# Attention in phases of 12 and 14 scores, with copies of scores and one arena of slots

## The chip, the cores and the metric

The kernel runs on one core of a Trainium2 chip. The metric is the device time of one execution in microseconds (us); smaller is better. Five engines work side by side, each with its own queue of instructions in order: TensorE (PE, the matmuls; PEld is its load of weights), ScalarE (ACT), VectorE (DVE), GpSimd (POOL) and SyncE (SP, which here starts the DMAs). They wait for one another through semaphores, and the queue of an engine never overtakes: what stands behind a waiting instruction waits too. TensorE writes to PSUM, a memory of eight banks of 128 x 512 floats; here seven of them hold scores and sums and one the second layer.

## The reference

Attention with 32 heads of 16 dimensions over 2048 tokens, and a token-mixing MLP, mixed by a gate:

```python
x = A_x                                                  # (1, 2048, 512)
g = sigmoid((x * gate_w).sum(-1, keepdims=True))
qkv = (x @ wqkv).reshape(B, S, 3, 32, 16).transpose(2, 0, 3, 1, 4)
p = softmax(einsum("bhqd,bhkd->bhqk", q, k) * 16 ** -0.5)
a = einsum("bhqk,bhkd->bhqd", p, v).transpose(0, 2, 1, 3).reshape(B, S, 512) @ wo
u = gelu(einsum("bsd,sf->bdf", layernorm(x), w1) + b1)   # F = 1792
b = (einsum("bdf,fs->bds", u, w2) + b2).transpose(0, 2, 1)
return g * a + (1 - g) * b
```

## The kernel before, in words

In front of the attention stand the layer norm, the projections to q, k and v and the MLP's first layer. They run at full array rows. Then comes the attention, three quarters of the time, and the MLP's second layer runs inside it. At the end stands a short stage of last outputs. All float32 products but the scores and AV are split in a high and a low part, three matmuls each.

The attention's work is counted in *units*. A unit is one score matmul (L868) of 128 keys by 512 queries of one head: it uses only 64 of the array's rows. On the other 64 rows a half of a second-layer or output matmul runs at the same time (L989, the list `beside`; its result is the bank `dn`). The scores land in one bank of PSUM, ACT takes their exponential and writes it to SBUF (`exponential`, L891), and `apply_v` (L826, here called AV) multiplies by V: two matmuls a unit, recorded as four instructions, all of a phase into one bank, which DVE then adds to the sums of the group in SBUF (L846, `ot`). The softmax's denominator comes out of AV as one more column, and the sums are divided at the end.

There are 32 groups of 64 units. The loop (L941 to L1017) goes through them in 8 phases of 8 units each, 256 phases in all. In a phase PE issues eight scores, six or eight of them with a partner, then AV of the *previous* phase's units; ACT takes two single exponentials and three of two banks each. `TURN` says for each of three kinds of phase which score goes to which of the seven banks, which exponentials are taken together, and which bank AV uses. In 21 groups one pair of scores is not given to ACT: DVE copies and scales it (L931) and computes the exponential in a polynomial, a few steps a phase (L907 to L920). DVE also carries out steps from the list `slow` (splits, divisions) where a phase has room. A memset on POOL (`token`, L993) in each phase keeps the order of the partners.

Nothing is left to a scheduler: the order on each queue is the order of the program. Waits come from what the framework tracks of the tiles; all seven banks are one tile, `banks`. Two functions add to that and take from it: `reads` and `writes` order an instruction behind those that last wrote or read its bank, and declare that there is no dependence on recent instructions that read another bank.

The output projection of the first half of the tokens is done in two passes of six matmuls: the first goes to DRAM (`part_d`) and is read again for the second.

Of the kernel before, what the change touches and what calls it, by code (L numbers as in the profile page):

```python
# [22 lines left out]
P = 128  # L23
# [52 lines left out]
def gated_mix(ctx: ExitStack, tc: tile.TileContext, a_x, a_wqkv, a_wo, b_w1, b_b1, b_w2, b_b2, gate_w, out):  # L76
# [415 lines left out]
    o_pool = ctx.enter_context(tc.tile_pool(name="o", bufs=1, reuse_waits="tile"))  # L492
    att_ctx = ExitStack()
    stk = att_ctx.enter_context(tc.tile_pool(name="stk", bufs=2, reuse_waits="tile"))
# [33 lines left out]
    def second_out(t, ps):  # L528
# [8 lines left out]
    QC = NB // 2  # L537

# [5 lines left out]
    TURN = [  # L544
# [3 lines left out]
    ]  # L548
# [4 lines left out]
    ptp_ctx = ExitStack()  # L553
    ptp = ptp_ctx.enter_context(tc.tile_pool(name="pt", bufs=7, reuse_waits="tile"))
# [3 lines left out]
    o_parts = {}  # L558
    wo_hi = o_pool.tile([P, ND, D], F32R, name="wo_hi")
    wo_lo = o_pool.tile([P, ND, D], F32R, name="wo_lo")  # L560
# [29 lines left out]
    def load_wo(k):  # L590
        raw = o_pool.tile([P, D], F32, name="o_sum")
        nc.sync.dma_start(raw, a_wo[k * P : (k + 1) * P, :])
        parts = wo_hi[:, k, :], wo_lo[:, k, :]
        slow.append((two + 1, lambda: split(*parts, raw, nc.vector.tensor_copy, nc.vector.tensor_tensor)))
# [6 lines left out]
    def open_end():  # L601

        nonlocal end
        u_ctx.close()
        wk_ctx.close()
        end = end_ctx.enter_context(tc.tile_pool(name="end", bufs=1, side="right", reuse_waits="tile"))

        least.append(end.tile([P, 1], F32, name="least"))
        nc.vector.tensor_reduce(least[0], ident.rearrange("p (j r) -> p j r", r=32)[:, :, DH], axis=AX.X, op=ALU.add)
        nc.vector.tensor_scalar(least[0], least[0], -1.0, 3e38, ALU.add, ALU.mult)  # L610
        nc.vector.tensor_scalar_add(least[0], least[0], LEAST_SUM)

    def load_wq():
        wq.extend(end.tile([P, 2, D], F32R, name=f"wq{n}") for n in range(2))
        raw = end.tile([P, 2, D], F32, name="wq_raw")
# [5 lines left out]
        slow.append((two + 2, lambda: split(wq[0], wq[1], raw, nc.vector.tensor_copy, nc.vector.tensor_tensor)))  # L621

    def fetch_o(half, k, pairs=4):
# [3 lines left out]
        pool, name, bufs = (end, str(k), 1) if half else (o_pool, "", 2)  # L627
        hi = pool.tile([P, QW], F32R, name=f"o_hi{name}", bufs=bufs)[: n * DH]
        lo = pool.tile([P, QW], F32R, name=f"o_lo{name}", bufs=bufs)[: n * DH]
        raw, rb = lo.bitcast(F32), hi.bitcast(F32)  # L630
        nc.sync.dma_start(raw, o_d[half][k][: n * DH])
        nc.sync.dma_start(rb, r_d[half][k][:n, None, :].broadcast_to([n, DH, QW]))

        at = two + (1 if two + 2 == NG * TWOS else 2)

        def divide(i):
            cols = slice(i * NB, (i + 1) * NB)
            o = o_pool.tile([P, NB], F32, name="o_sum")[: n * DH]
            nc.vector.tensor_mul(o, raw[:, cols], rb[:, cols])
            split(hi[:, cols], lo[:, cols], o, nc.vector.tensor_copy, nc.vector.tensor_tensor)  # L640

        slow.extend((at, lambda i=i: divide(i)) for i in range(2))
        o_parts[half, k] = hi, lo

    def o_matmuls(half, t, n, m):

        cols = slice(t % 8 * P, (t % 8 + 1) * P)
        for i in range(n, m):
            k, j = divmod(i, 3)
            hi, lo = (x[:, cols] for x in o_parts[half, k])  # L650
# [10 lines left out]
    def project(t, n, m):  # L661
# [3 lines left out]
        def load():  # L665
            if m == EARLY:
                row = end.tile([P, D], F32, name=f"base{t}")
            elif end and t % 2:
                row = end.tile([P, D], F32, name="row", bufs=3)
            else:  # L670
                row = out_pool.tile([P, D], F32, name="row", bufs=3)
            rows[t] = load_row(row, part_d[t] if n else bp_d[t])

        def step(i):
            if i == 0:
                box.extend((ps_dn.tile([P, D], F32, name="dn"), list(o_matmuls(t // NH, t, n, m))))

            def done():
# [3 lines left out]
                elif m != EARLY:  # L682
                    nc.sync.dma_start(part_d[t], rows[t])

            return box[0], *box[1][i], i == 0, i == m - n - 1, done if i == m - n - 1 else None

        return [(step, i) for i in range(m - n)], load
# [4 lines left out]
    TWOS = 4  # L692
    N_S = 8
    dense, calls = {}, {}

    def put(steps, at, sizes):
        for n in sizes:
            dense[at] = [steps.pop(0) for _ in range(n)]
            at += 1
# [6 lines left out]
    def put_outputs(tiles, n, m, at):  # L706
        for t in tiles:
            steps, load = project(t, n, m)
            call(at - (2 if m > 6 else 1), load)
            at = put(steps, at, [m - n])  # L710
        return at

    EARLY = 8
    part_d = [dram.tile([P, D], F32, name=f"part{t}") for t in range(NS)]
    for k in range(ND):
        call(3 * k + 2, load_wo, k)
    steps = second_layer(0)
    first, at = steps[:28], put(steps[28:], 0, [8, 6])
    for t in range(1, NS):
        at = put(second_layer(t), at, [8, 6] * 3 if t in (7, 14, 15) else [6] * 7)  # L720
        if t == 7:
            call(at - 7, fetch_o, 0, 0)
            call(at - 3, fetch_o, 0, 1)
            at = put_outputs(range(NH), 0, 6, at)
    call(at - 11, fetch_o, 0, 2)
    call(at - 7, fetch_o, 0, 3)
    call(at, open_end)
    done, at = at, put_outputs(range(NH), 6, 12, at)
    at = put_outputs(range(NH, NS), 0, EARLY, at)

    for k, n in enumerate((1, 3, 4)):
        call(done + n, fetch_o, 1, k)
    call(done + 9, load_wq)
    assert at == NG * TWOS
    call((NG - 1) * TWOS + 2, fetch_o, 1, 3, 3)

# [8 lines left out]
    recent = deque(maxlen=10)  # L745
# [11 lines left out]
    def writes(mm, bank, block=0, source=None):  # L757
# [3 lines left out]
        for ins in recent:  # L761
            if ins not in readers[bank] and ins is not source:
# [6 lines left out]


    EXTRA = *range(0, 11), *range(15, 25)
    EXTRA_PH = 2

    DVE_ROOM = 2.45

    two = 0
# [15 lines left out]
    def invert_sums(half, k, pairs):  # L792
# [14 lines left out]
        wait = 1 if (half, k) == (1, ND - 1) else 3  # L807
        later(wait, invert)
        later(wait + 1, store)

    def apply_v(late, bank):

        if not late:
            return
        g, units = late
        pairs = list(zip(*([u for u in units if u[2] == qb] for qb in range(2))))
        assert 2 * len(pairs) == len(units)
        av = banks[:, bank, :]
        taken = [0, 0]

        for pair in pairs:
            for i, c, qb, pt, act in pair:
                taken[qb] += 1
                for h in range(2):
                    j = 2 * qb + h
                    mm = nc.tensor.matmul(  # L826
                        av[32 * j : 32 * j + VC, i * QC : (i + 1) * QC],
                        v[:, c, g % NP * 2 + i, :],
                        pt[:, h * QC : (h + 1) * QC],
                        start=taken[qb] == 1,  # L830
                        stop=taken[qb] == len(pairs),
                    )
                    writes(mm, bank, j, act)

        there = {(i, qb) for i, _, qb, *_ in units}
# [13 lines left out]
    with tc.manual_schedule(engines=engines):  # L849
        kt, qt = {0: load_k(0)}, {0: load_q(0)}  # L850
        late, fence = None, None
# [9 lines left out]
        pt = None  # L861

        def score(grp, i, n, turn, exps, units, apart):

            c, qb = n // 2, (n + i) % 2
            bank = turn[len(units)]
# [9 lines left out]
            units.append([i, c, qb, None, None])  # L876
            for which in exps:
                if which[-1] == len(units) - 1:
                    if which == apart:
                        steps_of_exp(turn, units, which)  # L880
                    else:
                        exponential(turn, units, which)

        def exponential(turn, units, which):
            nonlocal pt
            if which[0] != 1:
                pt = ptp.tile([P, 2, NB], F32, name="pt")
            which = sorted(which, key=lambda m: turn[m])
            first, at = which == [1], [turn[m] for m in which]
            dst = pt[:, first : first + len(at), :]  # L890
            act = nc.scalar.activation(dst, banks[:, at[0] : at[-1] + 1, :], AF.Exp, scale=SCALE)  # L891
            reads(act, *at)
            for n, m in enumerate(which):
                units[m][3:] = dst[:, n, :], act

        def steps_of_exp(turn, units, which):

            z = o_pool.tile([P, QW], F32R, name="o_hi", bufs=2).bitcast(F32).rearrange("p (n c) -> p n c", n=2)
            box = []
# [281 lines left out]
```

## Time and profile before

| | us |
|---|---|
| median of the 3 runs | 1278.32 |
| lowest and highest | 1278.27 to 1279.09 |
| span of the profiled execution | 1276.0 |
| PE busy in it | 1266.6 (99%) |
| ACT busy in it | 1071.9 (84%) |
| DVE busy in it | 719.3 (56%) |
| first score of the first phase at | 303.45 |
| first score of the last phase at | 1253.09 |

For the profiled execution the page gives the span alone, from the first to the last instruction; it has no time of its own beside that. A row of a timeline gives the start, the length, the engine, the line, the operation with its output and inputs, and in brackets how long the engine had been idle and what released it. Ends of matmuls are modelled: in a row of them each is shown longer than the distance to the next. A group's row gives its count, its busy time, the mean of one in ns, and the idle time before it with what ended it.

### The profile page before, as it was taken

How to read it: one execution, taken by the hardware profiler on the slowest of the kernel's cores; microseconds unless marked ns; L12 is line 12 of the kernel's file. 1: busy time of each engine (PE TensorE's matmuls, PEld its weight loads, DVE VectorE, ACT ScalarE, POOL GpSimd, SP SyncE). 2: the span in 40 equal slices, each digit the busy share in tenths (PEclk: the TensorE clock that was granted, in tenths of full speed). 3: DMA queues.
4: the chain of work that ended last, by engine and by line, in shares of the span. 5: the costliest groups of instructions: out<-in, count | busy, mean ns of one | idle time of the engine just before them, and what ended most of it. 6: DMA issues, size and time to landing. Idle time of an engine off the chain costs nothing.

```text
span 1276.0 us, 33051 instructions
## 1 busy us (share of the span) xinstructions
PE 1266.6 (99%) x13278; PEld 801.2 (63%) x13278; DVE 719.3 (56%) x1329; ACT 1071.9 (84%) x1484; POOL 210.8 (17%) x435
## 2 busy tenths in 40 slices
PE   9999999999999999999999999999999999999998
PEld 7888888886555555555555555555555555555555
DVE  5675363528776766666634346676666662325425
ACT  3444343437999999999999999999999999999994
POOL 0210144454111111111110011111111111100000
PEclk9999999999999999999999999999999999999999
DMA  4497743328443333433555533333343345446721
GB/s 133 141 304 274 241 122 99 99 71 166 84 93 59 74 76 70 79 70 76 116 107 115 129 77 69 69 72 76 68 78 72 74 82 109 98 88 198 149 62 70
DMA packets 94641, 137.37 MB, mean 108 GB/s; under 512 B 16313, under 2 KB 55375, under 8 KB 91408
## 3 DMA queue, kind: packets, MB, share of 16 engines
q1 hardware_dynamic: 93904, 134.14, 44.8%
q8 instruction: 106, 1.74, 0.6%
q10 hardware_dynamic: 576, 1.05, 0.2%
q14 instruction: 55, 0.45, 0.1%
HBM read 99.10 MB, written 36.03 MB: 106 GB/s over the span
## 4 chain that ended last, share of the span: by engine, by line
PE 99%; DMA 0%; ACT 0%; SPq 0%; DVE 0%; issue 0%
PE s L826 37%; PE s L868 34%; PE acc L429 12%; PE acc L90 10%; PE dn L989 4%; PE pa L1060 1%; PE acc L201 1%; PE dn L857 0%; PE acc L268 0%; DMA x<-in_A_x_dram 0%; ACT pt L891 0%; PE pa L1069 0%; SPq L193 0%; DVE base L1082 0%; SPq L186 0%
## 5 line engine op out<-in xcount | busy, mean ns | idle before, releaser
L891 ACT ACTIVATE pt<-s 128x512 f32<-128x512 f32 (+1 forms) x1259 | 943.5, 962 | 10.0 <-PE s L868 4.3
L868 PE MATMUL s<-qs,ks 64*128 64x512 f32 x2048 | 493.9, 404 | 0.8 <-POOL token L993 0.5
L826 PE MATMUL s<-pt,v 128*17 128x256 f32 x8024 | 482.6, 381 | 0.0
L868 PEld LDWEIGHTS s<-qs,ks 64*128 64x128 f32 x2048 | 325.4, 184 | 168.7 <-ACT pt L891 91.0
L846 DVE TENSOR_TENSOR ot<-s,ot 128x256 f32<-128x256 f32 (+2 forms) x427 | 190.4, 447 | 348.9 <-PE s L826 271.6
L826 PEld LDWEIGHTS s<-pt,v 128*17 128x17 f32 x8024 | 210.4, 97 | 232.2 <-ACT pt L891 84.2
L989 PE MATMUL dn<-u_hi,w_hi 64*128 64x512 f32 x428 | 186.4, 436 | 0.0
L83 POOL TENSOR_TENSOR w_lo<-w_raw,w_hi 128x512 fp32r<-128x512 f32 (+1 forms) x126 | 149.7, 1189 | 167.3 <-ACT w_hi L82 107.3
L989 PE MATMUL dn<-u_lo,w_hi 64*128 64x512 f32 x430 | 169.8, 395 | 0.0
L989 PE MATMUL dn<-u_hi,w_lo 64*128 64x512 f32 x430 | 169.2, 394 | 0.0
L993 POOL MEMSET token<- 1x1 f32 x256 | 26.2, 102 | 779.4 <-PE dn L989 711.8
L913 DVE SCALAR_TENSOR_TENSOR row<-row,o_hi 128x512 f32<-128x512 f32 x168 | 116.6, 694 | 4.9
L82 ACT CAST w_hi<-w_raw 128x512 fp32r<-128x512 f32 (+1 forms) x67 | 38.1, 569 | 79.4 <-PE acc L429 58.9
L429 PE MATMUL acc<-h_hi,w_hi 128*128 128x512 f32 x224 | 87.1, 389 | 0.0
L429 PE MATMUL acc<-h_lo,w_hi 128*128 128x512 f32 x224 | 87.1, 389 | 0.0
L429 PE MATMUL acc<-h_hi,w_lo 128*128 128x512 f32 x224 | 87.1, 389 | 0.0
L989 PEld LDWEIGHTS dn<-u_hi,w_lo 64*128 64x128 f32 x430 | 79.3, 184 | 1.3
L989 PEld LDWEIGHTS dn<-u_lo,w_hi 64*128 64x128 f32 x430 | 79.4, 185 | 0.4
L989 PEld LDWEIGHTS dn<-u_hi,w_hi 64*128 64x128 f32 x428 | 78.6, 184 | 1.1
L90 PE MATMUL acc<-xt_hi,wc_hi 128*128 128x512 f32 x128 | 49.8, 389 | 0.0
L90 PE MATMUL acc<-xt_lo,wc_hi 128*128 128x512 f32 x128 | 49.8, 389 | 0.0
L90 PE MATMUL acc<-xt_hi,wc_lo 128*128 128x512 f32 x128 | 49.8, 389 | 0.0
(145 smaller groups left out, 1148.5 us busy)
## 6 DMA issues: line engine op xcount, KB each, us to landing
w_raw<-in_B_w_dram SPq DMA_DIRECT2D x96, 256.0 KB
ks<-kp SPq DMA_DIRECT2D x192, 128.0 KB
qs<-qp SPq DMA_DIRECT2D x256, 64.0 KB
qp<-pc SPq DMA_DIRECT2D x16, 768.0 KB
x<-in_A_x_dram SPq DMA_DIRECT2D x32, 256.0 KB
kp<-pc SPq DMA_DIRECT2D x16, 512.0 KB
w_raw<-in_B_w_dram SPq DMA_DIRECT2D x32, 128.0 KB
bp<-row SPq DMA_DIRECT2D x16, 256.0 KB
```

Of the source, the lines that this page charges most:

```text
L82: copy(hi, src)
L83: return sub(lo, src, hi.bitcast(F32), ALU.subtract)
L90: nc.tensor.matmul(ps, a, b, start=start and n == 0, stop=stop and n == last)
L201: nc.tensor.transpose(turns[t][:, k, :], xs[t][:, k * P : (k + 1) * P], ident)
L429: nc.tensor.matmul(p, a, b, start=first and k == 0, stop=last and k == 2)
L826: mm = nc.tensor.matmul(av[32 * j : 32 * j + VC, i * QC : (i + 1) * QC], v[:, c, g % NP * 2 + i, :], pt[:, h * QC : (h + 1) * QC], start=t ...
L846: reads(nc.vector.tensor_tensor(x, y, x, ALU.add), bank)
L868: mm = nc.tensor.matmul(banks[:, bank, :], kt[grp][rows, c * P : (c + 1) * P], qt[grp][rows, qb * NB : (qb + 1) * NB], start=True, stop=True,)
L891: act = nc.scalar.activation(dst, banks[:, at[0] : at[-1] + 1, :], AF.Exp, scale=SCALE)
L913: nc.vector.scalar_tensor_tensor(box[1], q or box[1], a, x, ALU.add, ALU.mult)
L989: mm = nc.tensor.matmul(ps, a[half], b[half], start=first and not second, stop=last and bool(second))
L993: fence = nc.gpsimd.memset(token, 0.0)
```

## The change

The 256 phases of 8 become 168: 122 of 12 units, 36 of 14 and 10 of 8 (the list `doubles`, in pairs). Scores are taken without regard to the border of a group, so a phase may hold units of two groups; AV then has two sets, the second into a bank of its own. `TURN` has new turns: in a phase of 12, ACT takes four singles and two triples; in a phase of 14, five singles and two triples. The scores left over (two of 12, three of 14) are copied by DVE out of PSUM (L1121) and exponentiated in place by ACT at the start of the next phase (`exponential_of_copies`, L1016); in some phases one of them goes to DVE's polynomial instead (46 units in all, before 42).

What ACT writes lies in one tile of 27 slots, `arena` (25 for exponentials). `take` looks for free slots that lie side by side, `give` frees a slot as AV is issued for it. Where the slots for the last triple are not free ahead of the phase's AV, the triple is *put off*: it is issued behind AV.

Further: 32 in place of 28 second-layer matmuls at full rows stand ahead of the first phase. The first half's outputs are computed in one pass of twelve (`fetch_tile` loads the parts for one tile of 128 tokens), with no `part_d`. `wo` is loaded and split where the buffers of the MLP are given up (`open_end`). The sums are opened two groups ahead, and q and k are loaded by the units done.

The core of the diff:

```diff
-    TURN = [
-        ((3, 4, 5, 6, 0, 1, 2, 3), ((0,), (1,), (2, 3), (4, 5), (6, 7)), 4),
-        ((5, 6, 0, 1, 2, 3, 4, 5), ((0,), (1,), (2, 3), (4, 5), (6, 7)), 6),
-        ((0, 2, 3, 1, 4, 5, 6, 0), ((0,), (1,), (2, 4), (5, 6), (3, 7)), 2),
-    ]
+    TURN = {
+        8: [
...
+        ],
+        12: [((0, 1, 4, 5, 6, 2, 3, 0, 1, 4, 5, 6), ((0,), (2,), (4,), (6,), (7, 8, 5), (9, 10, 11)), (1, 3), 3, 2)],
+        14: [
+            (
+                (0, 6, 5, 1, 4, 2, 0, 6, 3, 5, 4, 1, 2, 0),
+                ((0,), (2,), (3,), (5,), (8,), (10, 9, 7), (13, 11, 12)),
+                (1, 4, 6),
+                3,
+                6,
+            )
+        ],
+    }
...
+    arena = arena_pool.tile([P, SLOTS, NB], F32, name="arena")
...
-    first, at = steps[:28], put(steps[28:], 0, [8, 6])
+    AHEAD_OF_SCORES = 32
+    steps = second_layer(0)
+    first = steps[:AHEAD_OF_SCORES]
+    put(steps[AHEAD_OF_SCORES:], (12, 10))
+    for t in range(1, NS):
+        put(second_layer(t), (12, 10), (12, 10), (12, 10), (14, 12))
...
+        def exponential(units, turn, which, apart=False):
+            which = sorted(which, key=lambda m: turn[m])
+            if apart and sum(m < room_for[0] for m in stamps) < len(which):
+                return False
+            while which:
+                for n in range(len(which), 0, -1):
+                    slot = take(n)
+                    if slot is not None or not apart:
+                        break
+                if slot is None:
+                    return False
+                now, which = which[:n], which[n:]
+                span = [turn[m] for m in now]
+                dst = arena[:, slot : slot + n, :]
+                act = nc.scalar.activation(dst, banks[:, span[0] : span[-1] + 1, :], AF.Exp, scale=SCALE)
+                reads(act, *span)
+                for at, m in enumerate(now):
+                    units[m].source = act
+                    hold(units[m], slot + at, phase + 1)
+            return True
+
+        def exponential_of_copies(copied):
+            while copied:
...
+                dst = arena[:, slot : slot + n, :]
+                act = nc.scalar.activation(dst, dst, AF.Exp, scale=SCALE)
+                for unit, at in copied[:n]:
+                    unit.source = act
+                    hold(unit, at, phase)
+                del copied[:n]
...
+                exponential_of_copies(copied)
...
+                for m, i in enumerate(order):
+                    units.append(score(i, turn[m]))
+                    for which in exps:
+                        if max(which) == m and (put_off or not exponential(units, turn, which, which != exps[-1])):
+                            put_off.append(which)
+                    if m in copies:
+                        bank = banks[:, turn[m], :]
...
+                            slot = copies_at[len(copied)]
+                            ins = nc.vector.tensor_copy(arena[:, slot, :], bank)
+                            copied.append((units[m], slot))
+                        reads(ins, turn[m])
...
+                sets = matched(phase)
...
+                for (grp, pairs), bank in zip(sets, (av_bank, other_bank)):
+                    while there and put_off and any(bank in [turn[m] for m in which] for which in put_off):
+                        assert exponential(units, turn, put_off.pop(0), apart=True), (phase,size,len(sets),sorted(stamps),room_for,[(g,len(p)) for g,p in sets])
...
+                    there.append((grp, bank, apply_v(grp, pairs, bank)))
+                while put_off:
+                    assert exponential(units, turn, put_off.pop(0), apart=True)
...
+                for grp, bank, where in there:
+                    add_sums(grp, bank, where)
+                    if summed[grp] == GROUP:
+                        store_sums(grp)
+                        open_sums(grp + 2)
```

More of the change, by code (lines that the diff above doesn't have):

```diff
@@ L588, in later, with whenever @@
         soon.setdefault(phase + phases, []).append((what, args))
[L590 to L594, printed above, removed]
+    def whenever(phases, cost, what):
+        slow.append((phase + phases, cost, what))
     end_ctx = ExitStack()
@@ L614, in load_wq @@
         wq.extend(end.tile([P, 2, D], F32R, name=f"wq{n}") for n in range(2))
-        raw = end.tile([P, 2, D], F32, name="wq_raw")
+        assert all(m in stamps for m in range(WQ_AT, SPARE))
+        raw = arena[:, WQ_AT : WQ_AT + 2, :]
         nc.gpsimd.memset(raw, 0.0)
@@ L755, in reads, with writes @@
                 tc.add_manual_dep(ins.ins, mm.ins.name, SYNC, reason="the bank is written")
-    def writes(mm, bank, block=0, source=None):
+    def writes(mm, bank, block=0, sources=()):
         if readers[bank]:
@@ L766, in writes, with open_sums @@
         readers[bank].clear()
[L771 to L776, printed above, removed]
+    def open_sums(g):
+        if g < NG:
+            sums[g] = out_pool.tile([P, NB], F32, name="ot")
+            nc.gpsimd.memset(sums[g], 0.0)
     def store_sums(g):
@@ L804, in store, with __init__ @@
             inverted.add((half, k))
[L807 to L817, printed above, removed]
+        later(1, invert)
+        later(2, store)
+    class Unit:
+        def __init__(self, grp, i, c, qb):
+            self.grp, self.i, self.c, self.qb = grp, i, c, qb
+            self.p = self.source = self.slot = None
@@ new lines, in gated_mix, with matched @@
+    waiting = {g: [] for g in range(NG)}
+    summed = {g: 0 for g in range(NG)}
+    def matched(until):
+        out = []
+        for g in sorted(sums):
+            can = [u for when, u in waiting[g] if when <= until]
+            pairs = list(zip(*([u for u in can if u.qb == qb] for qb in range(2))))
+            if pairs:
+                gone = {id(u) for pair in pairs for u in pair}
+                waiting[g] = [(when, u) for when, u in waiting[g] if id(u) not in gone]
+                summed[g] += 2 * len(pairs)
+                out.append((g, pairs))
+        return out
@@ L835, in apply_v @@
-        there = {(i, qb) for i, _, qb, *_ in units}
+                        av[32 * j : 32 * j + VC, u.i * QC : (u.i + 1) * QC],
+                        v[:, u.c, g % NP * 2 + u.i, :],
+                        u.p[:, h * QC : (h + 1) * QC],
+                        start=n == 0,
+                        stop=n == len(pairs) - 1,
+                    )
+                    writes(mm, bank, j, (u.source,))
+                give(u.slot)
+        return {(u.i, u.qb) for pair in pairs for u in pair}
@@ L836, in apply_v, with add_sums @@
+    def add_sums(g, bank, there):
+        av = banks[:, bank, :]
         if len(there) == 4:
@@ L937, in without @@
[L937 to L953 removed]
+            return Unit(grp, i, c, qb)
@@ L1017, in gated_mix @@
-                late = grp, units
-        assert not slow and not soon and not exp_steps
+                    beside = [step(*args) for step, *args in steps]
+                if last_phase:
+                    nc.vector.tensor_scalar_max(sums[NG - 1], sums[NG - 1], least[0])
+                if size == 8:
+                    turn, exps, copies, av_bank, other_bank = TURN[8][turns % 3]
+                    turns += 1
+                else:
+                    turn, exps, copies, av_bank, other_bank = TURN[size][0]
@@ new lines, in gated_mix @@
+                mark[0] = clock[0]
+                exponential_of_copies(copied)
+                by_dve = copies[:1] if phase % 2 == 0 and at[second] % (GROUP // 2) < DVE_UNTIL else ()
+                for_act = [m for m in copies if m not in by_dve]
+                copies_at = []
+                while len(copies_at) < len(for_act):
+                    for n in range(len(for_act) - len(copies_at), 0, -1):
+                        slot = take(n)
+                        if slot is not None:
+                            copies_at.extend(range(slot, slot + n))
+                            break
@@ L1035, in gated_mix @@
         divided(0)
-        apply_v(late, TURN[(2 * two + second + 1) % len(TURN)][-1])
+        (_, pairs), = matched(phase + 1)
+        assert all(u.i for pair in pairs for u in pair) and summed[NG - 1] == GROUP
+        last_bank = TURN[8][turns % 3][3]
+        add_sums(NG - 1, last_bank, apply_v(NG - 1, pairs, last_bank))
         divided(1)
```

425 lines of the change are left out of this document (231 added, 194 removed), and 3 rows, old and new, of the table TURN.

## The prediction

> **What bounds the kernel now.** I read the page's first part and its chain, then the attention stretches by window, then single phases in the timeline.
>
> ```profile
> span 1276.0 us, 33051 instructions
> PE 1266.6 (99%) x13278; PEld 801.2 (63%) x13278; DVE 719.3 (56%) x1329; ACT 1071.9 (84%) x1484; POOL 210.8 (17%) x435
> ```
> ```profile
> core 0: us, PE busy (x) PEld busy (x) DVE busy (x) ACT busy (x) POOL busy (x), PEclk, DMA share, GB/s
> 500.00:600.00 100.00, 100.00 (x1248) 57.25 (x1244) 70.03 (x130) 98.86 (x134) 14.35 (x39) 1.00 0.37 70
> 1100.00:1200.00 100.00, 100.00 (x1239) 57.82 (x1232) 41.88 (x85) 99.94 (x134) 5.39 (x31) 1.00 0.53 134
> 1253.00:1276.00 23.00, 16.63 (x164) 11.54 (x160) 13.00 (x25) 5.90 (x9) 1.40 (x2) 0.95 0.27 96
> ```
>
> The page says PE, at 99%, but in the attention stretch ACT is just as full: 98.9 and 99.9 of 100 us. The weight loads show who is late when PE pauses:
>
> ```profile
> engine line waited for: us in total, times, longest us
> PEld s L868 <- ACT pt L891: 91.0, 214, 0.6
> PEld s L826 <- ACT pt L891: 84.2, 250, 0.4
> ```
>
> Both score (L868) and AV (L826) loads wait for exponentials, never over 0.6 us. So ACT and PE are balanced: one full ACT instruction takes 99.94/134 = 0.746 us, five of them (two singles, three pairs) 3.73, and that is a phase:
>
> ```profile
> 303.45 0.49 PE L868 MATMUL s<-qs,ks 64*128 64x512 f32 x1
> 303.98 0.60 ACT L891 ACTIVATE pt<-s 128x512 f32<-128x512 f32 x1
> 1253.09 0.50 PE L868 MATMUL s<-qs,ks 64*128 64x512 f32 x1
> ```
>
> These are the first score of the first phase, its first exponential and the first score of the last phase, 255 phases later: 949.64 us, 3.72 each.
>
> **Prices.** Exponentials by shape:
>
> ```profile
> L891 ACT ACTIVATE pt<-s 128x1024 f32<-128x1024 f32 x747 | 740.2, 1146 | 0.0
> L891 ACT ACTIVATE pt<-s 128x512 f32<-128x512 f32 x512 | 302.9, 694 | 10.0 <-PE s L868 4.3 <-PE dn L989 2.0
> ```
>
> The recorded means overlap, so I take their difference, 1146 − 694 = 0.452 us for each further 512 columns, and solve 2a + 3(a + 0.452) = 3.73 for the single: a = 0.475, a pair 0.927, a triple 1.379. With an empty pipe the single above took 0.60: 0.125 more for the fill. On PE:
>
> ```profile
> 1048.07 0.50 PE L868 MATMUL s<-qs,ks 64*128 64x512 f32 x1
> 1048.41 0.39 PE L868 MATMUL s<-qs,ks 64*128 64x512 f32 x1
> 1048.64 0.39 PE L868 MATMUL s<-qs,ks 64*128 64x512 f32 x1
> 1050.12 1.92 PE L826 MATMUL s<-pt,v 128*17 128x256 f32 x32
> 1051.97 0.49 PE L868 MATMUL s<-qs,ks 64*128 64x512 f32 x1
> 401.31 1.49 PE L826 MATMUL s<-pt,v 128*17 128x256 f32 x24
> 402.73 0.50 PE L868 MATMUL s<-qs,ks 64*128 64x512 f32 x1
> 740.51 0.61 PE L826 MATMUL s<-pt,v 128*17 128x256 f32 x8
> 741.05 0.49 PE L868 MATMUL s<-qs,ks 64*128 64x512 f32 x1
> 741.25 0.42 DVE L846 TENSOR_TENSOR ot<-s,ot 128x256 f32<-128x256 f32 x1 [2.39 <-PE s L826]
> ```
>
> A paired score costs 0.23 (1048.41 to 1048.64). An AV block takes 1.85 to the next score with 8 units (32 instructions) and 1.42 with 6: 0.215 a unit and 0.13 besides. A whole phase with a second-layer partner for all 8 scores is 3.90 (1048.07 to 1051.97). And the row that matters most: an instruction that waits for the *last* AV matmul starts 0.20 after the next phase's first score (741.25 against 741.05).
>
> **What longer phases save.** 255 phase changes become 167. That is worth PE time, 3.90 − 7 × 0.23 − 8 × 0.215 = 0.57 less the first score's own 0.23, so 0.34 × 88 = 30 us, but ACT has to follow. In the changed program ACT exponentiates 2002 units in 1301 instructions, before 2006 in 1259. At 0.452 a unit and 0.023 an instruction (0.475 − 0.452) that is 934.8 against 935.7 us: nothing. ACT already sets the pace, so the most that is there is the phases' 949.6 less 934.8: 15 us.
>
> **The put-off triple.** In a phase of 12 ACT does four singles and two triples, and two units are copied to the arena by DVE and exponentiated in place at the start of the next phase. The second triple often finds no free slots and is put off: issued behind that phase's AV, which frees them. The plan does this in 139 of 168 phases (in 7 of them with both triples). In the built program each of these triples waits for a PE semaphore value that only the last AV matmul of its phase raises: PE raises its semaphore once in 161 of 167 AV blocks, at the block's end. The slots needed are freed by unit 5.7 on average of some 12. The reason appears to be that all banks are one tile, so that the triple, which reads banks 4 to 6, is ordered behind AV's writes to bank 3. Queued behind it on ACT, in order, are the exponential of the copies and all singles of the next phase. And AV of the next phase needs the copies' exponential (its units) and the last single (it reads bank 3, where AV writes). So ACT and PE alternate where they had overlapped. Per phase of 12, from a possible first score to the next:
>
> - triple starts: 0.20; triple with fill: 1.379 + 0.125 = 1.50
> - exponential of the copies E: 0.475, 0.927 or 1.379 for 1, 2, 3 units
> - four singles: 1.90 (five in a 14: 2.375; two in an 8: 0.95)
> - to AV 0.04, AV 0.13 + 0.215 V
>
> So 3.77 + E + 0.215 V; 0.475 more for a 14. The 0.04 is the gap from a score's end to the exponential behind it (303.45 + 0.49 to 303.98). The first triple runs beside AV, 2.66 us long, and ends inside it; then ACT is idle. PE's third score waits for the triple's bank too, inside the same chain.
>
> Counts and means are those of the built program:
>
> - 106 phases of 12 behind a put-off, E 0.863, V 12.28: 7.274 each, 771.0
> - 30 of 14, E 1.048, V 12.8: 4.245 + 1.048 + 2.752 = 8.045, 241.4
> - 3 of 8: 18.5
> - 7 second put-off triples × 1.379: 9.7
> - not behind one: 16 of 12, ACT-bound (1.90 + 2.76 + 0.72 = 5.4): 86.4; 6 of 14, PE-bound (13 × 0.23 + 14 × 0.215 + 0.33 = 6.33): 38.0; 6 of 8 ahead of the last phase × 3.89: 23.3
> - in 45 phases AV has two groups, and the second one's bank is read by the first triple: 28 stall, 1.379 less 0.215 per unit of the first set, 15 in sum
>
> Sum 1203.3, against 949.6 for the 255: +253.7.
>
> **The rest.** Four more full-row second-layer matmuls ahead of the scores:
>
> ```profile
> 297.17 6.35 PE dn L857 x28
> ```
>
> 6.35/28 = 0.227 each, +0.9. DVE gets 306 copies and 4 more exponentials of ten instructions, and has 307 sums in place of 427:
>
> ```profile
> L846 DVE TENSOR_TENSOR ot<-s,ot 128x256 f32<-128x256 f32 (+2 forms) x427 | 190.4, 447 | 348.9 <-PE s L826 271.6
> L913 DVE SCALAR_TENSOR_TENSOR row<-row,o_hi 128x512 f32<-128x512 f32 x168 | 116.6, 694 | 4.9
> L931 DVE TENSOR_SCALAR o_hi<-s 128x512 f32<-128x512 f32 x42 | 27.1, 686 | 15.0 <-PE s L868 14.9
> ```
> ```profile
> L846 DVE TENSOR_TENSOR ot<-s,ot 128x512 f32<-128x512 f32 x35 | 24.2, 692 | 51.7 <-PE s L826 50.1 <-ACT pt L891 1.6
> ```
>
> Copies 306 × 0.686 = 210 (priced by the nearest row with the same source and size, L931), exponentials at most 4 × 10 × 0.694 = 28, sums 91 whole at 0.692 and 216 smaller at (190.4 − 24.2)/392 = 0.424: 155 in place of 190. That is some 203 more on 719, in a longer span: about 60%. DVE was 42 to 70% busy and mostly waited for AV, so I cost it at nothing; a copy or sum that frees a bank late by 0.1 us a phase would be 14. The first half's outputs in one pass of twelve are the same matmuls with fewer DVE steps and DMAs; the loads of k and q two groups ahead, and the fewer POOL tokens, sit on queues with room (POOL 17%, DMA 0.37 to 0.53): nothing.
>
> **Sum.** 1276.0 + 253.7 + 0.9 = 1530.6 span. The runs' median, 1278.32, is 2.3 above the span, and I keep that: **1533 us**.
>
> **Rivals.**
> *The triple waits only for its slots.* Were it released by unit k, it could start 0.04 + 0.215 k + 0.13 + 0.20 after the last single, and the first triple keeps ACT busy for 1.379 of that: late by 0.215 k − 1.01 where that is positive, 48 us summed over the counts of k in the built program. On the floor of 1276.0 − 15 + 0.9 + 2.3 = 1264, with the 15 of the two-group phases: 1327. For it speaks that AV and triple use different banks; against it that the built program has no PE signal in the middle of AV. Chance 0.04. The Trainium skill, "PSUM — Partial Sum Buffer", section "PSUM bank collisions raise a hardware error", asks for a semaphore by bank and quadrant, by bank in its simple version. By that rule the triple need not wait for writes into another bank, and this rival's time would hold; no run shown here tells.
> *The other side: faster.* If the wait were hidden (ACT so far ahead that its triple would have come no sooner than AV's end), longer phases give their 15 us: 1264. It decides if the wait costs under 0.1 us a phase (139 × 0.1 = 14). Against it: ACT at 99.9 of 100 us has no slack in which to stand idle. Chance 0.04, 0.01 of it near no change.
> *PE slows.* PE would pause some 3 us of every 7.3. In the profile the clock is 1.00 in full stretches and 0.95 in the last one, where PE is busy 16.63 of 23. At 0.95, AV's 2.66 × 139 = 370 us grow by 19: within the range. Were AV to take twice as long, 1533 + 370 = 1903. Chance 0.03. The Trainium skill, "TensorE: Matmul & The Clock Gate", section "A second HAM failure mode: psum-queue depth-cycling", tells of a kernel whose clock swung because PE idled briefly between groups while it cycled through PSUM banks; the 0.95 is the only sign of it here.
>
> **Numbers.**
>
> ```profile
> L82 ACT CAST pc<-acc 128x512 fp32r<-128x512 f32 x32 | 18.6, 585 | 23.8 <-PE acc L90 19.2 <-DMA qp<-pc 4.6
> L82 ACT CAST h_hi<-hf 128x512 fp32r<-128x512 f32 x16 | 9.8, 617 | 7.1 <-DVE hf L348 4.5 <-DMA x<-in_A_x_dram 2.5
> ```
>
> Main case 0.89. Its bounds: the triple's start 0.20 or 0.11 (−12); triples and copies 0.05 either way (±14); late DVE (+14); two-group stalls 0 to 30 (±15); exponentials from the arena 0.03 an instruction dearer, as casts of one size are from SBUF (617 ns) against PSUM (585), over some 170 of them (+5): 1485 to 1581, given as 1488 to 1580. The rivals hold 0.11, so the range stays with these. Faster by over 0.2%, about what a measurement of this kernel can tell: 0.03; within it 0.01; slower 0.96.
>
> **What would show it.** In the profile after: put-off triples starting 0.2 us behind the next phase's first score, released by PE's AV; ACT busy near 0.8 and idle for 1.3 to 1.6 us before each such triple; AV waiting for ACT; phases of 12 some 7.3 long and of 14 some 8.0; the AV block as before, 0.054 us an instruction; granted clock near 1. Wrong if these triples start in the middle of AV, if ACT stays near 99%, or if phases of 12 last about 5.5.

## The result and the profile after

The changed kernel takes 1595.72 us (median of 4 runs, 1593.46 to 1598.1) against 1278.3 before: ratio 1.2483, interval 1.2465 to 1.25. The forecast was 1533 with a range to 1580. The direction and most of the size came as forecast; the time lies 16 us beyond the range.

The page's first part and three stretches of the profiled execution (stretch, its length, busy time of PE, PEld, DVE, ACT and POOL with counts, granted clock, DMA share, GB/s), the last of them the output phases:

```profile
span 1591.7 us, 32727 instructions
PE 1371.3 (86%) x13274; PEld 828.3 (52%) x13274; DVE 920.2 (58%) x1547; ACT 1088.0 (68%) x1526; POOL 203.4 (13%) x343
```
```profile
328.50:775.00 446.50, 382.00 (x4406) 210.06 (x4406) 269.81 (x456) 351.95 (x483) 47.36 (x102) 1.00 0.31 59
775.00:1220.30 445.30, 377.08 (x4354) 206.93 (x4346) 268.81 (x455) 344.63 (x468) 45.35 (x99) 1.00 0.31 58
1220.30:1474.80 254.50, 195.34 (x2013) 98.82 (x2013) 141.92 (x236) 173.75 (x236) 4.71 (x30) 0.93 0.41 86
```

ACT was full before; it is now busy 352 of 446 us, 79%, and PE 86%. Neither is the bound: they wait for each other. The waits of the changed kernel, ACT's line first, then the weight loads':

```profile
ACT arena L1002 <- PE s L926: 270.9, 141, 5.1
...
PEld s L972 <- ACT arena L1002: 320.4, 448, 3.5
PEld s L926 <- ACT arena L1002: 77.9, 185, 2.2
```

141 times ACT waits for AV (L926), 271 us in all; the forecast had 139 put-off triples. Two phases from the timeline, ACT's rows and PE's:

```profile
701.98 1.45 ACT L1002 ACTIVATE arena<-s 128x1536 f32<-128x1536 f32 x1 [1.99 <-PE s L926]
703.32 0.62 ACT L1016 ACTIVATE arena<-arena 128x512 f32<-128x512 f32 x1
703.84 3.40 ACT L1002 ACTIVATE arena<-s 128x512 f32<-128x512 f32 x5
708.43 1.45 ACT L1002 ACTIVATE arena<-s 128x1536 f32<-128x1536 f32 x1 [1.19 <-PE s L926]
```
```profile
699.72 2.13 PE L926 MATMUL s<-arena,v 128*17 128x256 f32 x36
701.78 0.49 PE L972 MATMUL s<-qs,ks 64*128 64x512 f32 x1
...
702.12 0.39 PE L972 MATMUL s<-qs,ks 64*128 64x512 f32 x1
...
703.48 0.49 PE L972 MATMUL s<-qs,ks 64*128 64x512 f32 x1 [0.97 <-ACT arena L1002]
...
705.95 2.35 PE L926 MATMUL s<-arena,v 128*17 128x256 f32 x40
708.24 0.50 PE L972 MATMUL s<-qs,ks 64*128 64x512 f32 x1
```

AV ends, the next phase's first score starts at 701.78, and the put-off triple at 701.98: 0.20 later, the forecast's figure. Behind it come the copies' exponential, four singles and a triple, and again 1.19 us of nothing until AV ends. PE's third score waits for the triple. The phase lasts 6.46 us; the formula gives 3.77 + 0.475 + 0.215 x 10 = 6.40.

By stage, in the profiled execution, against the same sum:

| | forecast | measured |
|---|---|---|
| first score at | 304.4 | 309.3 |
| phases 0 and 1 | 10.8 | 19.3 |
| phases 2 to 121 (second layer) | 875.3 | 891.8 |
| phases 122 to 151 (outputs) | 224.2 | 254.4 |
| phases 152 to 166 | 93.4 | 93.9 |

The rest of the span, 23.0 from the last phase's first score, is that of before (22.9). So the sum falls short by 13 us at the start, by 16 in the longest stage (2%) and by 30 in the output phases.

### The profile page after: what moved, and what is told of

It is laid out like the page before. It is cut to its first block, busy times and chain, and to the rows that moved or that the text cites. A ratio compares the mean times of both kernels' runs of the same rounds, so it can differ in the third digit from the quotient of the medians.

```text
span 1591.7 us, 32727 instructions
## 1 busy us (share of the span) xinstructions
PE 1371.3 (86%) x13274; PEld 828.3 (52%) x13274; DVE 920.2 (58%) x1547; ACT 1088.0 (68%) x1526; POOL 203.4 (13%) x343
## 4 chain that ended last, share of the span: by engine, by line
PE 73%; ACT 18%; DMA 3%; issue 2%; DVE 2%; SPq 2%; ACTq 0%; POOL 0%; POOLq 0%; DVEq 0%
PE s L926 27%; PE s L972 24%; ACT arena L1002 17%; PE acc L429 10%; PE acc L90 8%; PE dn L1127 2%; ACT arena L1016 1%; DMA ks<-kp 1%; SPq L515 1%; DMA s<-ot 1%; PE pa L1214 0%; PE acc L201 0%; PE acc L268 0%; DVE ot L949 0%; PE dn L960 0%
## 5 line engine op out<-in xcount | busy, mean ns | idle before, releaser
L1002 ACT ACTIVATE arena<-s 128x512 f32<-128x512 f32 (+2 forms) x1142 | 830.7, 824 | 309.2 <-PE s L926 270.9
L972 PE MATMUL s<-qs,ks 64*128 64x512 f32 x2048 | 581.1, 435 | 183.9 <-ACT arena L1002 165.1
L972 PEld LDWEIGHTS s<-qs,ks 64*128 64x128 f32 x2048 | 338.3, 190 | 430.7 <-ACT arena L1002 320.4
L926 PE MATMUL s<-arena,v 128*17 128x256 f32 x8192 | 487.7, 385 | 16.5 <-ACT arena L1002 16.3
L949 DVE TENSOR_TENSOR ot<-s,ot 128x256 f32<-128x256 f32 (+2 forms) x307 | 153.8, 503 | 345.9 <-PE s L926 312.3
L926 PEld LDWEIGHTS s<-arena,v 128*17 128x17 f32 x8192 | 223.0, 98 | 250.9 <-ACT arena L1002 77.9
L1121 DVE COPY arena<-s 128x512 f32<-128x512 f32 x306 | 207.7, 688 | 102.3 <-PE s L972 92.5
L1034 DVE SCALAR_TENSOR_TENSOR arena<-arena 128x512 f32<-128x512 f32 x230 | 163.7, 712 | 6.3
L1016 ACT ACTIVATE arena<-arena 128x1024 f32<-128x1024 f32 (+2 forms) x159 | 163.1, 1027 | 0.0
L1127 PE MATMUL dn<-wo_hi,o_hi 64*128 64x512 f32 x112 | 51.5, 460 | 12.2 <-POOL token L1133 12.2
```

What stands on the lines that cost most here:

```text
L926: mm = nc.tensor.matmul(av[32 * j : 32 * j + VC, u.i * QC : (u.i + 1) * QC], v[:, u.c, g % NP * 2 + u.i, :], u.p[:, h * QC : (h + 1) * QC] ...
L949: reads(nc.vector.tensor_tensor(x, y, x, ALU.add), bank)
L972: mm = nc.tensor.matmul(banks[:, bank, :], kt[grp][rows, c * P : (c + 1) * P], qt[grp][rows, qb * NB : (qb + 1) * NB], start=True, stop=True,)
L1002: act = nc.scalar.activation(dst, banks[:, span[0] : span[-1] + 1, :], AF.Exp, scale=SCALE)
L1016: act = nc.scalar.activation(dst, dst, AF.Exp, scale=SCALE)
L1034: nc.vector.scalar_tensor_tensor(box[1], box[1] if q is None else q, a, x, ALU.add, ALU.mult)
```

## The experiments

**e1: the triple waits only for its slots.** The first rival, built:

```diff
+                    av_mms.append((mm, bank, u.slot))     # in apply_v
...
                 reads(act, *span)
+                if apart:
+                    for mm, b, at in av_mms:
+                        if b not in span and not slot <= at < slot + n:
+                            tc.declare_no_dep(act.ins, mm.ins, reason="another bank")
```

> The changed kernel with one addition: a put-off triple is declared independent of those AV matmuls of its phase that write another bank and read none of the slots it takes. Order of all queues, copies, slots and phases stay. Theory (the triple's wait for the last AV matmul makes ACT and PE take turns): the put-off phases go back to the ACT-bound pace but for the 48 us of triples whose slots come free late; of the 61 us by which the span exceeded the forecast (start, output phases) most stays. 1595.7 - 206 = 1390, between 1360 and 1410; ACT's wait for AV falls from 271 us to about 50. Rival (the pauses of PE slow its clock, or the DVE copies and longer phases cost the time): 1570 to 1600.

1450.58 us, 145 less (ratio to before 1.1344, interval 1.1325 to 1.1363). The waits in its trace:

```profile
ACT arena L1004 <- PE s L927: 84.2, 94, 3.0
ACT arena L1004 <- PE s L974: 61.6, 75, 6.5
```

ACT's wait for AV fell from 271 to 84 us by this edit alone. The theory holds, the number doesn't: 60 us more stayed than I had said. ACT's wait for AV stayed at 84 where 50 had been expected, and other waits have grown: PE's scores wait 24.5 us for late sums (8.5 in the changed kernel), and its second-layer and output matmuls 28.2 us for POOL's token (12.2). How the 60 us divide among them is not shown.

**e2: the same wait put into the kernel before.**

```diff
-            for which in exps:
+            for which in exps[:-1]:
...
                 apply_v(late, av_bank)
+                if exps[-1] == alone:
+                    steps_of_exp(turn, units, exps[-1])
+                else:
+                    exponential(turn, units, exps[-1])
```

> The kernel before with one change: in each phase the exponential of the last two scores is issued behind AV in place of ahead of it. No longer phases, no copies, no arena. Theory: this alone brings the wait into the old kernel: 0.20 + 1.05 (pair with fill) + 0.95 (two singles, the second of which frees AV's bank) + 0.04 + 0.13 + 8 x 0.215 = 4.09 us a phase in place of 3.72, times 255: +94, 1372, between 1350 and 1395. Rival (a wait there is hidden, since ACT has the first triple or pairs to run beside AV): 1278 to 1285.

1391.12 us (1.0883, 1.0865 to 1.0901): 113 us for 255 phases, 0.44 each, where 0.37 had been worked out. In the kernel before, ACT's list of waits has no row for AV; now it has one, nearly once a phase:

```profile
ACT pt L891 <- PE s L826: 92.5, 234, 1.1
```

So an exponential issued behind AV is enough, without long phases, copies or arena.

**e3: all phases of 8.** `put` gets (8, 6) and (8, 8) throughout, two pairs of phases without partners stand ahead of the outputs as in the change, and one load of output parts stands three pairs of phases earlier.

> The changed kernel with all 256 phases of 8 units; arena, pass of twelve outputs, placement in memory and start as in the changed kernel. With phases of 8 nothing is copied, nothing goes to DVE's exponential and no exponential is put off; ACT takes all 2048 units. Theory: 2048 x 0.452 + 1280 x 0.023 = 955 us of ACT in place of 936, +20, and some 13 us lost at the first scores as in the changed kernel: 1305, between 1290 and 1330. Rival (arena, loads and outputs cost much of the change's time): 1400 or more.

1565.98 us: neither theory. There is no put-off triple in it, and the trace names another wait:

```profile
PE dn L1127 <- POOL token L1133: 190.1, 30, 15.7
...
POOL ot L862 <- DMA o<-ot: 178.3, 16, 13.2
...
POOL ot L862 <- DMA s<-ot: 173.9, 14, 20.9
```

POOL sets the sums of the group after next to zero (L862) in the buffer that is just being stored. It waits for the store; the token of the second-layer matmuls stands behind it on POOL, and PE waits for the token. The forecast had put the tokens "on queues with room" without asking what they are queued behind.

**e4: slots freed sooner.** As e1; where a triple is put off, AV's units are sorted so that three neighbouring slots come first.

> As the run with the slot wait, and where a triple is put off the units of AV are reordered so that three neighbouring slots are free first: the triple now waits for unit 3.5 on average, before 5.5. Theory: most of the 48 us of late triples goes, 1345, between 1310 and 1370. Rival (the triple is late for another reason than its slots): no faster than the run with the slot wait alone.

1426.68 us, 24 less than e1; ACT's wait for AV 37.6 in place of 84.2. Of the 48 us of late triples half came back.

**e5 and e6: the sums opened later,** in the changed kernel and with phases of 8.

```diff
-                        open_sums(grp + 2)
+                        if grp + 2 < NG:
+                            later(4, open_sums, grp + 2)
```

> The changed kernel with one edit: the sums of the group after next are opened (a memset on POOL) four phases after the old ones are stored, not at once. The memset writes the buffer that is being stored, so on POOL it waits for the store, and the token that orders the second-layer matmuls stands behind it. Theory (both waits are real, and in the changed kernel the put-off triple hides most of the second): PE waited 12 us for the token there, so 1580, between 1565 and 1590. Rival (the memset is no cost): 1593 to 1598.

> All phases of 8, as in the run before at 1566, with the same later opening of the sums. Theory: there PE waited 190 us for the token and lost clock besides, and nothing else in the arena, the loads or the outputs is dear: 1320, between 1295 and 1370. Rival (the loads and stores of the new output pass are the cost): 1480 or more.

e5 1597.88 us, no gain: the expectation failed. e6 1350.34, 216 less than e3. With phases of 8, POOL's wait was on the path; in the changed kernel the same edit takes one wait away while another grows:

```profile
PE s L972 <- ACT arena L1002: 170.3, 153, 3.0
PE s L972 <- DVE ot L949: 18.4, 8, 5.0
```

The token is gone from this list (it had 12.2 us), and the wait for sums has risen from 8.5 to 18.4; what stands behind that, e13 and e17 show.

**e7 and e8: repairs together.** e7 is e4 with the later opening and `shift_rows` of the second k buffer on POOL. e8 adds the q and k buffers ahead of the arena in memory and the larger set of AV first.

> Slot wait and order of AV (1426.7 alone), with the later opening of the sums and the second k buffer's constant rows set by POOL in place of DVE in the first phase. Theory: 33 us of PE's waits for the token and some 8 at the start go, and part of the 24 for late sums: 1375, between 1350 and 1395. Rival: the waits only change their name, 1410 or more.

> As the run before it in this call, with the q and k buffers placed in memory ahead of the arena (in the changed kernel the first scores wait 5.1 us for a load of q that waits for a buffer of the MLP), and in phases with two sets of AV the larger set first (the second set's bank is read by the first triple: 15 us by the forecast). Theory: 10 to 20 us less than that run. Rival: no difference over 3 us.

1415.09 and 1402.48 us. e7 brought 12 where 50 was expected, e8 13 more as expected. The second-layer stage is at 747 us in e8 (892 in the changed kernel, 763 in e4).

**e9 and e10: four rooms for the output tiles,** loaded four tiles ahead and divided two or three phases after, with the start's two edits; in the changed kernel, and with phases of 8.

> The changed kernel with the put-off triples as they are, and two edits aside from them: four rooms in place of two for the first half's output tiles, each loaded four tiles ahead and divided two or three phases after its load in place of one; and q and k buffers placed ahead of the arena, the second k buffer's constant rows set by POOL. Theory (the 61 us by which the span exceeded the forecast lie at the start, 13, and in the output phases, 30, where DVE's division waits for its loads and the sums stand behind it): the second-layer stage stays at 890, the start loses some 8 us and the output phases some 17: 1570, between 1555 and 1580. Rival (the excess is spread over all stalled phases): 1590 or more.

> All phases of 8 with the later opening of the sums (1350.3), and the same two edits. Theory: PE's 50 us of waits for late sums in the output phases go, and some 6 at the start: 1297, between 1285 and 1315, what 2048 units on ACT cost. Rival (the output pass of twelve is dearer for its matmuls' order or its DMA traffic): 1335 or more.

e9 1582.2 us, 13.5 less; e10 1344.48, where 1297 was expected. In e9 the start (first score and phases 0 and 1) got 7 us shorter and the output phases 8; two phases still took 14.1 and 14.2. DVE's rows of one of them:

```profile
1278.29 1.48 DVE L1120 COPY arena<-s 128x512 f32<-128x512 f32 x2
1288.02 0.69 DVE L698 TENSOR_TENSOR arena<-o_lo,o_hi 128x512 f32<-128x512 f32 x1 [8.24 <-DMA o_hi<-r]
...
1291.72 0.68 DVE L948 TENSOR_TENSOR ot<-s,ot 128x512 f32<-128x512 f32 x1
```

The division of the second half's parts (L698) waits 8.24 us for a load issued one phase before, and the sums (L948), which free AV's bank, stand behind it.

**e11 and e12: DVE.** All repairs and the four rooms; e11 with 0.7 us less room for DVE's other steps in a phase, e12 with no exponential on DVE.

> Slot wait, order of AV, later opening, start, larger set first (1402.5 together), with the four rooms, and DVE's room for other steps 0.7 us smaller in each phase of the second-layer stage, so that the sums are added sooner (PE waited 55 us for them). Theory: 10 to 17 us from the output phases and 20 to 35 from the sums: 1360, between 1340 and 1380. Rival (DVE's lateness only covers another wait of the long phases): 1385 or more.

> As the run before it in this call, but with the room as in the change and no exponential on DVE at all (some 46 units fewer there, 46 more on ACT: 21 us of ACT, some 300 us of DVE). Theory: if late sums hold the long phases, they now come in time and ACT is full in the second-layer stage: 1360, between 1340 and 1380. Rival (the long phases lose the time in ACT's order, not to DVE): 1400 or more.

1405.65 and 1372.29 us (one more execution of e12's kernel, on record as e14: 1372.75). Less room was no help: the second-layer stage was 756 us, 9 more than in e8. Without exponentials on DVE it was 729, although ACT has 46 units more; ACT is there 98% busy:

```profile
500.00:600.00 100.00, 97.61 (x1216) 56.62 (x1204) 45.11 (x88) 97.48 (x128) 12.91 (x28) 1.00 0.40 76
700.00:800.00 100.00, 98.79 (x1228) 56.93 (x1226) 44.52 (x86) 98.55 (x125) 12.18 (x28) 1.00 0.38 69
```

**e13, e15, e16: the division three phases after its load,** in e9, e10 and e12 (in e10 for one more load of parts: `k < 3`); **e17** is e13 with the later opening too.

```diff
-            whenever(2 if n < P // DH else 1, 1.75, lambda i=i: divide(i))
+            whenever(3 if k < 2 else 2 if n < P // DH else 1, 1.75, lambda i=i: divide(i))
```

> The changed kernel with its put-off triples, the four rooms and the start's edits (1582.2), and the second half's parts divided three phases after their load in place of one. Theory: the two phases of 14 us go back to 7.3, 13.7 us in all: 1568, between 1562 and 1574; the sums of the output phases come to within 12 us of the forecast. Rival (the loads are late because of the DMA queue's own order and the wait only moves on): 1578 or more.

> All phases of 8 with the later opening, the four rooms, the start's edits (1344.5), and the parts divided three phases after their load. Theory: PE's 48 us of waits for late sums go: 1297, between 1285 and 1315. Rival (SyncE's queue, in which these loads stand behind those of q, k and a finished row, makes them late whatever the division's phase): 1330 or more.

> All repairs without exponentials on DVE (1372.3), and the parts divided three phases after their load. Theory: 10 to 15 us of the output phases go: 1360, between 1352 and 1366; the long phases then stand above the kernel before even with neither wait. Rival: 1370 or more.

> The changed kernel with its put-off triples, the four rooms, the start's edits and the later divisions (1582.2), and with the later opening of the sums. Theory (two waits of the same length lie over one another, so that taking away either alone brought nothing): the phases of 14 us go to 7.3, 13.4 us in all: 1569, between 1563 and 1575. Rival (a third wait stands behind them, or the loads themselves are the limit): 1579 or more.

e13 1582.23 us: nothing, where 1568 was expected. e15 1315.21, 29 less, at the upper edge of its range; e16 1345.08, 27 less, more than expected; e17 1576.68, 5.5 less, where 13 was expected. In e13 the same two phases took 14.1 and 13.9 us, and their wait had its other name:

```profile
1289.34 0.79 PE L1126 MATMUL dn<-wo_hi,o_hi 64*128 64x512 f32 x1 [6.28 <-POOL token L1132]
```

With both edits (e17) the two phases take 7.74 us each. So two waits of nearly the same length lay over one another, and taking away either alone brought nothing. The whole gain is smaller than expected: the second-layer stage of e17 took 4 us longer than that of e13, its start 2, and another output phase 3; why, no run tells.

None of these versions beats the kernel before. e16 and e15 compare long phases and phases of 8 with most of the waits repaired, both with all 2048 units on ACT: 1345 against 1315 us. In each, two phases still take far longer than their neighbours: 14.0 and 14.7 us in e16, 18.5 and 10.4 in e15.

## Why the prediction was right, and where it failed

**The put-off triple** was the main cause of the loss, and its price in a usual phase was right. Put into the old kernel the same wait costs 113 us; made to wait for its slots alone in the changed one, it gives back 145, and with AV reordered 169. The 106 phases of 12 behind a put-off took 784.2 us by the trace, 7.40 each; the formula gives 7.27, and 7.39 with the stalls of two groups and the second triples that fall on them.

**Phases of 14** took 9.14 us against 8.05 by the formula, 8.26 with stalls and second triples. This is mostly a shift, as the first score behind one shows:

```profile
730.84 1.45 ACT L1002 ACTIVATE arena<-s 128x1536 f32<-128x1536 f32 x1 [1.98 <-issue]
```
```profile
732.34 0.50 PE L972 MATMUL s<-qs,ks 64*128 64x512 f32 x1 [1.62 <-ACT arena L1002]
```

A 14's triple reads bank 0, where the next phase's first score goes; that phase starts 1.6 us later, and a phase of 12 behind a 14 is shorter by as much (most took 6.90 us, where the formula gives 8.59). The prediction had the triple of every phase start behind the next phase's first score, so it had the order wrong here; the time comes back in the phases behind.

**The step that failed is "the rest"**, priced at 0.9 us. The loads of q and k, the outputs' loads and the tokens were costed at nothing because their queues had room, and the range had no bound for them either. What counts is not how full a queue is, but what stands in it behind a wait. At the start (13 us), PE waits 5.1 us for a load of q, and then for copies that stand behind other DVE work; between the two its clock is half, and scores come every 0.43 us in place of 0.23:

```profile
PE s L972 <- DMA qs<-qp: 5.1, 1, 5.1
PE s L972 <- DVE arena L1121: 3.2, 1, 3.2
```
```profile
307.20:320.70 13.50, 9.58 (x38) 5.85 (x38) 7.50 (x9) 7.83 (x11) 0.09 (x1) 0.50 0.72 173
```

In the output phases (30 us), three phases took 12.2, 13.4 and 13.6 us, 17 more than the formula gives them: there the division waits for its loads and the token for a store. The second put-off triple in a phase was mis-sized too: 1.379 us was put down for each of the 7, but the phases around them (120 to 122, 134 to 136, 144 to 146, 150 to 153, 158 and 159) exceed their sum by 15 us, 2 for each of the 7, and some 13 of these 15 lie in the output phases. With the division and the opening of the sums both moved, e17 still exceeds the sum there by 14 us. The rest of the 61 us, some 15, is spread over the second-layer stage, and no run takes it apart.

**The clock** cuts across these terms. The forecast had it near 1. In the profiled execution it is 0.977, half for 75 us in all, which is at most 37 us of full-clock work; most of these stretches lie at the start and in the output phases. How much of the 61 us they cost no run separates, for the pauses and the slow stretches behind them come together.

**The rivals.** The first (wait for the slots alone) was no description of this program, but its repair could be made; its 1327 took the loads at nothing too, and e1 is at 1451. The faster one is out. The slower clock came, though not where I looked for it: in the second-layer stage it is 1.00, and half in one stretch of 3.4 us alone. PE's pauses there are 133 us in 120 phases, 1.1 each, and not the 3 us of every 7.3 that the rival took. The bounds listed below the rivals add up to 1492 at the lower end, not to 1485; the measured time lies at the other end.

**The floor.** That long phases could save no more than 15 us, since ACT sets the pace, is not contradicted: no run with long phases comes below e15 or below the kernel before. It is not measured either, since two phases of e16 still lose time.

## What to carry to other kernels

An instruction issued behind another engine's block waits for what the program's semaphores say, not for what it needs: look up in the built program which instruction raises the value that it waits for. Where a kernel has one engine full, price an edit by what its instructions stand behind on each queue; a queue as little used as POOL's, busy 13% of e3, can hold the path through one wait. When a repair brings nothing, look whether the same stretch now waits under another name, and take both away before the first is called harmless.

## What the hardware showed

PE's clock fell to half behind some of its pauses, and the length of a pause alone does not tell behind which. Three stretches of the changed kernel, each behind a pause of PE (1.91, 2.97 and 2.97 us), and the first scores in them:

```profile
795.30:798.60 3.30, 3.30 (x20) 2.53 (x16) 1.69 (x3) 2.52 (x6) 0.00 (x0) 0.50 0.00 0
...
1213.10:1218.00 4.90, 4.90 (x55) 3.11 (x58) 3.73 (x6) 3.32 (x6) 0.09 (x1) 1.00 0.03 10
...
1412.80:1416.30 3.50, 3.45 (x18) 2.71 (x20) 1.59 (x3) 3.47 (x6) 0.00 (x0) 0.53 0.00 0
```
```profile
794.16 0.49 PE L972 MATMUL s<-qs,ks 64*128 64x512 f32 x1 [1.91 <-ACT arena L1002]
...
795.58 0.62 PE L972 MATMUL s<-qs,ks 64*128 64x512 f32 x1
...
796.01 0.62 PE L972 MATMUL s<-qs,ks 64*128 64x512 f32 x1
...
1213.09 0.50 PE L972 MATMUL s<-qs,ks 64*128 64x512 f32 x1 [2.97 <-ACT arena L1002]
...
1213.43 0.39 PE L972 MATMUL s<-qs,ks 64*128 64x512 f32 x1
...
1213.66 0.39 PE L972 MATMUL s<-qs,ks 64*128 64x512 f32 x1
...
1412.85 0.65 PE L972 MATMUL s<-qs,ks 64*128 64x512 f32 x1 [2.97 <-ACT arena L1002]
...
1413.30 0.62 PE L972 MATMUL s<-qs,ks 64*128 64x512 f32 x1
...
1413.73 0.62 PE L972 MATMUL s<-qs,ks 64*128 64x512 f32 x1
```

At half clock scores come every 0.43 us, otherwise every 0.23. A pause of 2.97 us was followed by half the clock at 1412.85 and by none at 1213.09; one of 1.91 us was enough at 794.16. In the trace's record of the clock the stretches at half last 3.41 us or a multiple of it (13.65 at the start, 3.41 or 6.83 behind that; the last one ends with the kernel), and their starts lie multiples of 3.41 us apart: from 795.22 to 1221.89 it is 125 times. So it seems to count where a pause falls among steps of 3.41 us, and not only how long it is; this is inferred from these stretches, and no run tests it.

In the output phases the clock is 0.93 of 254.5 us, at most 18 us of work. The Trainium skill, "TensorE: Matmul & The Clock Gate", section "What's actually happening", gives half the clock after an idle window of about 3.4 us and the full one after a busy window as long; the trace agrees with the length of the stretches (3.41 us), but shorter pauses, of 2.97 and 1.91 us, were already enough here. The section on depth-cycling on the same page of the Trainium skill, weighed in the prediction, finds no support in the second-layer stage: pauses of 1.0 us in some 60 of its 120 phases, and of 1.2 to 1.6 us in some 40 more, left the clock at 1.00. In the output phases two slow stretches, from 1341.4 and from 1430.1 us, came behind pauses of no more than 1.7 us; whether that is what the section describes, no run tells.
